# All thirteen steps of a block's attention rows on DVE from block 4 on, in a window attention followed by a SiLU MLP

## The chip, the cores and the metric

The kernel runs on one core of one Trainium2 chip. The metric is the device time of one execution in microseconds, the median of several runs. A core has five engines with queues of their own, each worked off strictly in order: PE (TensorE, with its weight loads as PEld), DVE (VectorE), ACT (ScalarE), POOL (GpSimd) and SP (SyncE, which here only starts DMAs).

## The reference

```python
w = softmax(weight_gen)                 # over 7 taps, per token and head: (4, 4096, 8, 7)
x_pad = 6 zero rows, then x             # (4, 4096, 192), 8 heads of 24 columns
a[s, h] = sum over k of w[s, h, k] * x_pad[s + k, h]       # k = 0 .. 6
h = a @ w_in                            # 192 -> 2048
out = (h * sigmoid(h)) @ w_out          # 2048 -> 192, 16384 tokens
```

The attention rows `a` of one block take seven multiplications (one for each tap, with the softmax weight spread over a head's 24 columns) and six additions: thirteen elementwise operations.

## The kernel before, in words

The 16384 tokens are 128 tiles of 128, worked in 32 blocks of four tiles. Each block goes through eight pairs of hidden slices: 256 blocks-times-pairs in all, numbered through; "pair n" is one of them, and pairs 8b to 8b+7 belong to block b. For each pair there is
- `mm1` on PE (L570): the first product into a PSUM buffer `h`. There are two such buffers, taken in turn.
- `act` on ACT (L582): SiLU in place in `h`; then `upper` on ACT (L593): the high f16 half of it into a ring in SBUF.
- `lower` on DVE (L597): the low f16 half, from `h` and the high half. It is the last reader of `h`; `mm1` of pair n+2 needs it done.
- the second product on PE (L611 for blocks 1 to 5, L636 and L640 from block 6 on), some pairs behind. `mm1` is ahead of it by three pairs at first and by nine at the end (`lead`); where the lead grows by one, two `mm1` follow each other without a second product between them.
- every second pair (from block 6 on) the output steps: L681 on ACT, L682 and L684 on DVE, and a DMA out.

Beside this runs the preparation of later blocks. `prep_steps` (L460) makes the attention rows of a block: multiplications (L472) and additions (L478) on tiles of 128 x 768 f32, then `hi` on ACT (L445) and `lo` on DVE (L448) split the sum into f16 halves, and `turned` lets a DMA transpose them. In blocks 1 to 3 DVE does all thirteen operations. From block 4 on POOL does taps 0 to 2 (three multiplications, two additions) and DVE taps 3 to 6 (four multiplications, three additions) and one addition that brings both sums together: eight on DVE.

The softmax of the weights is made by chunk; from block 4 on a chunk is four blocks. `softmax_steps` (L362): maximum on DVE (L369), subtraction (L372) on POOL, exponential on ACT (L376, with two table loads around it), sum on DVE (L380), reciprocal on DVE (L384, L385), and `norm`, the multiplication with the reciprocal, on POOL (L388). (Chunk 3 has the POOL steps on DVE.)

The order within an engine is written out by hand: `START` gives each preparation step a due time in half pairs, counted from `u0 = (b - 2) * 16` of its block, `chain` enters the steps, and `drain(u)` in the main loop emits what is due, once ahead of a pair's `lower` (even number) and once behind it (odd number). Steps with a fraction are emitted at the next drain.

Of the kernel before, what the change touches and what calls it, by code (L numbers as in the profile page):

```python
# [50 lines left out]
    "any_x": (-39, -27, -15, -11, -4.5, 3, 4, 5),  # L51
    "early": (-5, -41),
    "b3v": (11, 11, 13, 13, 15, 17, 17, 18, 19, 20.5, 20.5, 21, 21, 22.5, 23, 23),
    "b4v": (10, 12, 13, 14.5, 16, 17, 18.5, 20, 22.5, 23, 23),
    "any_p": (11.25,) * 5,
    "any_v": (11, 11.5, 13, 14, 15, 17, 18.5, 20, 22.5, 23, 23),
    "prep": (12.5,),
    "load": (0,),
}
# [19 lines left out]
def kernel(  # L79
# [362 lines left out]
    def split(xs, acc, c, ts):  # L442

        def hi():
            nc.scalar.activation(out=xs[:, ts, 0:D], in_=acc, func=AF.Copy, scale=sc[c, "up"])  # L445

        def lo():
            nc.vector.scalar_tensor_tensor(out=xs[:, ts, D:2 * D], in0=acc, scalar=sc[c, "up"],  # L448
                                           in1=xs[:, ts, 0:D], op0=ALU.mult, op1=ALU.subtract)
        return hi, lo  # L450

    def turned(b, xs):
        def turn():
            xt[b] = xt_p.tile([P, TB, NG, P], F16, tag="xt", name=f"xt{b}")
            nc.sync.dma_start_transpose(out=xt[b].rearrange("p t k n -> p (t k) n"),
                                        in_=xs.rearrange("p t n -> p (t n)"))
            swapped(b, slice(0, TB), (nc.sync, nc.sync))
        return turn

    def prep_steps(b, share):  # L460

        c = chunk_of[b]
        r0 = b * TB - chunks[c][0]
        tags = [0, 1, 1] + [2, 3, 3, 3] if share else [0] + [1 + k % 3 for k in range(K - 1)]
        tiles = [pr_p.tile([P, TB, D], F32, tag=f"pr{n}", name=f"pr{b}_{n}") for n in range(4)]
        pr = [tiles[n] for n in tags]

        def mul(eng, k):
            def f():
                xin = x_t[c][:, r0 + k:r0 + k + TB, :].rearrange("p t (h g) -> p (t h) g", g=G)  # L470
                wv = w_t[c][:, r0 * H:(r0 + TB) * H, k:k + 1].to_broadcast([P, TB * H, G])
                eng.tensor_tensor(out=pr[k].rearrange("p t (h g) -> p (t h) g", g=G),  # L472
                                  in0=xin, in1=wv, op=ALU.mult)
            return f

        def add(eng, k, l):
            def f():
                eng.tensor_tensor(out=pr[k], in0=pr[k], in1=pr[l], op=ALU.add)  # L478
            return f

        def ordered(eng, ks):
            fs = [mul(eng, ks[0])]
            for k in ks[1:]:
                fs += [mul(eng, k), add(eng, ks[0], k)]
            return fs

        pool = ordered(nc.gpsimd, range(share)) if share else []
        steps = ordered(nc.vector, range(share, K)) + ([add(nc.vector, share, 0)] if share else [])
        xs = xs_p.tile([P, TB, 2 * D], F16, tag="xs", name=f"xs{b}")
        hi, lo = split(xs, pr[share % K], c, slice(0, TB))  # L490
        return pool, steps, [hi, lo, turned(b, xs)]
# [210 lines left out]
    def at(u, f):  # L702
        todo.append((u, len(made), f))
        made.append(f)
# [7 lines left out]
    def chain(name, fs, u0=0):  # L712
        steps = START[name][-len(fs):]
        for u, f in zip(steps, fs):
            at(u0 + u, f)

    win, wout = moe_w_in.bitcast(I32), moe_w_out.bitcast(I32)
    with tc.manual_schedule():
# [118 lines left out]
        for c in range(2, NC):  # L837
            u0 = (chunks[c][0] // TB - 2) * NF
# [26 lines left out]
        for b in range(2, NB):  # L865
            u0 = (b - 2) * NF

            def prep(b=b, u0=u0):
                pool, steps, last = prep_steps(b, 0 if b < 4 else 3)
                if b > 2:  # L870
                    chain("any_p", pool, u0)
                chain(f"b{b}v" if b < 5 else "any_v", steps + last, u0)
            at(START["prep"][0] if b == 2 else u0 - 1, prep)

# [101 lines left out]
```

## Time and profile before

| | before |
|---|---|
| median of 3 runs | 1031.17 us (1030.92 to 1033.29) |
| the profiled execution | 1031.08 us, span of its trace 1029.3 us |
| PE busy | 1024.7 us (100% of the span) |
| DVE busy | 788.0 us (77%) |
| ACT busy | 728.3 us (71%) |
| POOL busy | 278.3 us (27%) |

The span runs from the first to the last instruction that the trace shows; 1.8 us of the execution lie around it. Busy shares are averages over the span. A busy PE is not proof of PE at its peak, since the ends of its matmuls are modelled; where PE stands still is seen better from the starts of its instructions. Durations of DVE, ACT and POOL overlap a little: the next one can begin before the end that the trace gives for the last, so what an operation costs its engine is read from start to start.

### The profile page before, as it was taken

To read this page: it belongs to the slowest core of one execution; us is meant where nothing else is said; L and a number is where in the kernel's file an instruction comes from. 1 tells how busy PE (TensorE), PEld (TensorE's weight loads), DVE (VectorE), ACT (ScalarE), POOL (GpSimd) and SP (SyncE) were. 2 spreads that over 40 slices of the span, in tenths; PEclk is the share of its full clock that TensorE was granted. 3 is DMA by queue.
4 is the path that set the end of the run, shared out by engine and by line. 5 is a ranking of instruction groups with operands and counts; after the bars stand their busy time and mean duration, and the time that the engine had idled before them with its cause. 6 is when DMAs were issued, how large, how long until landed. Compare 5 with 4: busy or idle time off the path is not lost.

```text
span 1029.3 us, 30061 instructions
## 1 busy us (share of the span) xinstructions
PE 1024.7 (100%) x13492; PEld 862.9 (84%) x13492; DVE 788.0 (77%) x925; ACT 728.3 (71%) x795; POOL 278.3 (27%) x178
## 2 busy tenths in 40 slices
PE   9999999999999999999999999999999999999998
PEld 7699777788888888888888888888888888888888
DVE  8899866778887777977878778787787877777543
ACT  7988668767786677766787666876668766666662
POOL 1000443433412334312344213343123433123000
PEclk9999999999999999999999999999999999999999
DMA  9441411124112241013221141111312210111100
GB/s 264 138 134 32 151 33 48 48 43 147 15 42 48 50 140 35 22 48 108 82 47 25 32 150 48 39 48 25 134 48 47 41 47 10 47 48 40 47 18 25
DMA packets 71771, 66.74 MB, mean 65 GB/s; under 512 B 51421, under 2 KB 65370, under 8 KB 70618
## 3 DMA queue, kind: packets, MB, share of 16 engines
q1 hardware_dynamic: 71642, 64.83, 23.8%
q8 instruction: 105, 1.72, 0.7%
q14 instruction: 24, 0.20, 0.1%
HBM read 27.85 MB, written 12.58 MB: 39 GB/s over the span
## 4 chain that ended last, share of the span: by engine, by line
PE 99%; DMA 0%; DVE 0%; SPq 0%; issue 0%; ACT 0%; DVEq 0%
PE h L570 47%; PE acc L636 26%; PE acc L640 13%; PE acc L611 8%; PE h L561 2%; PE acc L623 2%; DMA xc<-in_x_dram 0%; PE sum L519 0%; PE acc L649 0%; PE turn L534 0%; DVE pr L513 0%; DVE ringed L528 0%; DVE pr L524 0%; DVE ringed L513 0%; SPq L337 0%
## 5 line engine op out<-in xcount | busy, mean ns | idle before, releaser
L597 DVE SCALAR_TENSOR_TENSOR ringed<-h,gup,ringed 128x1024 f16<-128x1024 f32 x248 | 317.2, 1279 | 213.3 <-ACT ringed L593 213.2
L582 ACT ACTIVATE h<-h,inv 128x1024 f32<-128x1024 f32 x248 | 269.7, 1088 | 266.5 <-PE h L570 264.8
L636 PE MATMUL acc<-wo,ringed 64*128 64x384 f16 x3312 | 433.7, 322 | 0.0
L570 PEld LDWEIGHTS <-w 64*128 64x128 f16 x4464 | 326.1, 94 | 110.0
L640 PE MATMUL acc<-wo,ringed 64*128 64x192 f16 x3312 | 417.7, 243 | 0.0
L570 PE MATMUL h<-xu,w 64*128 64x512 f16 x2232 | 308.4, 376 | 0.0
L570 PE MATMUL h<-xt,w 64*128 64x512 f16 x2232 | 308.4, 376 | 0.0
L593 ACT ACTIVATE ringed<-h,gup 128x1024 f16<-128x1024 f32 x248 | 276.3, 1114 | 8.0
L636 PEld LDWEIGHTS <-ringed 64*128 64x128 f16 x3312 | 259.1, 94 | 20.6
L640 PEld LDWEIGHTS <-ringed 64*128 64x128 f16 x3312 | 259.2, 94 | 11.9
L472 POOL TENSOR_TENSOR pr<-xc,wc 128x768 f32<-128x768 f32 x84 | 136.7, 1641 | 323.5 <-DVE pr L478 227.4
L472 DVE TENSOR_TENSOR pr<-xc,wc 128x768 f32<-128x768 f32 x133 | 129.1, 974 | 1.0
L478 DVE TENSOR_TENSOR pr<-pr,pr 128x768 f32<-128x768 f32 x130 | 128.6, 989 | 0.6
L478 POOL TENSOR_TENSOR pr<-pr,pr 128x768 f32<-128x768 f32 x56 | 111.6, 1993 | 4.4
L611 PEld LDWEIGHTS <-ringed 64*128 64x128 f16 x1920 | 83.9, 94 | 6.1
L611 PE MATMUL acc<-wo,ringed 64*128 64x192 f16 x1920 | 87.7, 243 | 0.0
L682 DVE SCALAR_TENSOR_TENSOR t<-acc,od,t 128x384 f32<-128x384 f32 x103 | 62.7, 609 | 7.8 <-ACT t L681 7.8
L681 ACT ACTIVATE t<-acc,od 128x384 f32<-128x384 f32 x103 | 59.0, 573 | 9.8 <-PE acc L640 9.8
L684 DVE TENSOR_TENSOR o<-t 128x192 f32<-128x192 f32 x103 | 56.1, 545 | 3.6
L448 DVE SCALAR_TENSOR_TENSOR xs<-pr,xup,xs 128x768 f16<-128x768 f32 x31 | 56.5, 1822 | 0.8 <-ACT xs L445 0.8
L388 POOL TENSOR_TENSOR wc<-wc,ws 128x896 f32<-128x896 f32 x6 | 11.1, 1844 | 110.5 <-DVE ws L385 110.5
L372 POOL TENSOR_TENSOR wc<-wc,wm 128x896 f32<-128x896 f32 x6 | 10.5, 1754 | 84.2 <-DVE wm L369 84.2
(101 smaller groups left out, 346.6 us busy)
## 6 DMA issues: line engine op xcount, KB each, us to landing
xc<-in_x_dram SPq DMA_DIRECT2D x7, 2112.0 KB, 9.3
xu<-xt SPq DMA_DIRECT2D x62, 192.0 KB, 3.0
out_dram<-o SPq DMA_DIRECT2D x61, 192.0 KB, 2.7
wc<-in_weight_gen_dram SPq DMA_DIRECT2D x7, 448.0 KB, 3.8
ringed<-in_moe_w_out_dram SPq DMA_DIRECT2D x8, 384.0 KB, 6.8
ringed<-in_moe_w_in_dram SPq DMA_DIRECT2D x14, 192.0 KB, 7.1
xc<-in_x_dram SPq DMA_DIRECT2D x1, 1344.0 KB, 10.5
xc<-in_x_dram SPq DMA_DIRECT2D x2, 384.0 KB, 5.1
```

Of the source, the lines that this page charges most:

```text
L448: nc.vector.scalar_tensor_tensor(out=xs[:, ts, D:2 * D], in0=acc, scalar=sc[c, "up"], in1=xs[:, ts, 0:D], op0=ALU.mult, op1=ALU.subtract)
L472: eng.tensor_tensor(out=pr[k].rearrange("p t (h g) -> p (t h) g", g=G), in0=xin, in1=wv, op=ALU.mult)
L478: eng.tensor_tensor(out=pr[k], in0=pr[k], in1=pr[l], op=ALU.add)
L570: nc.tensor.matmul(h[:, i], w16[rows, part, p, g], x_in[rows, :, k, :], start=n == 0, stop=n == NT9 - 1)
L582: nc.scalar.activation(out=h, in_=h, func=AF.Silu, scale=sc[chunk_of[b], "inv"])
L593: nc.scalar.activation(out=g_t[b, p][:, 0], in_=h_t[b, p], func=AF.Copy, scale=sc[chunk_of[b], "gup"])
L597: nc.vector.scalar_tensor_tensor(out=g[:, 1], in0=h_t.pop((b, p)), scalar=sc[chunk_of[b], "gup"], in1=g[:, 0], op0=ALU.mult, op1=ALU.subtract)
L611: nc.tensor.matmul(acc_t[b, i, t // 2][:, t % 2, :], g[rows, t * P:(t + 1) * P], wo16[rows, place(f), part], start=f == ORDER[0] and t % 2 ...
L636: nc.tensor.matmul(acc_t[b, t, i], gh_t[b, f][rows, t * P:(t + 1) * P], wo16[rows, place(f)], start=f == 0, stop=False, skip_group_check=True)
L640: nc.tensor.matmul(acc_t[b, t, i][:, 0, :], gl_t[b, f][rows, t * P:(t + 1) * P], wo16[rows, place(f), 0], start=False, stop=False, skip_gr ...
L681: nc.scalar.activation(out=t1, in_=acc_t[b, t, 0], func=AF.Copy, scale=sc[c, "od"])
L682: nc.vector.scalar_tensor_tensor(out=t1, in0=acc_t[b, t, 1], scalar=sc[c, "od"], in1=t1, op0=ALU.mult, op1=ALU.add)
```

## The change

From block 4 on `prep_steps(b, 0)` is called instead of `prep_steps(b, 3)`: DVE does the seven multiplications and six additions of a block by itself, as it did in blocks 1 to 3, and POOL none of them. The list of due times for POOL goes, and the two for DVE have sixteen entries (thirteen operations, `hi`, `lo`, `turned`) instead of eleven; the first is 9 instead of 10 or 11, the last three stay. POOL keeps L372, L388 and the maxima over partitions (L166).

```diff
-    "b4v": (10, 12, 13, 14.5, 16, 17, 18.5, 20, 22.5, 23, 23),
-    "any_p": (11.25,) * 5,
-    "any_v": (11, 11.5, 13, 14, 15, 17, 18.5, 20, 22.5, 23, 23),
+    "b4v": (9, 10, 11, 11.5, 13, 13.5, 15, 15.5, 17, 17.5, 19, 19.5, 21, 22.5, 23, 23),
+    "any_v": (9, 10, 11, 11.5, 13, 13.5, 15, 15.5, 17, 17.5, 19, 19.5, 21, 22.5, 23, 23),
...
             def prep(b=b, u0=u0):
-                pool, steps, last = prep_steps(b, 0 if b < 4 else 3)
-                if b > 2:
-                    chain("any_p", pool, u0)
+                _, steps, last = prep_steps(b, 0)
                 chain(f"b{b}v" if b < 5 else "any_v", steps + last, u0)
```

## Rows read from the trace of the kernel before

**Rows 1.** Chain that ended last: share of the span by engine and line.

```profile
PE h L570 47%; PE acc L636 26%; PE acc L640 13%; PE acc L611 8%; PE h L561 2%; PE acc L623 2%; DMA xc<-in_x_dram 0%; PE sum L519 0%; PE acc L649 0%; PE turn L534 0%; DVE pr L513 0%; DVE ringed L528 0%; DVE pr L524 0%; DVE ringed L513 0%; SPq L337 0%
```

**Rows 2.** Page's groups: line, engine, tiles, count, busy us, mean ns, idle before.

```profile
L597 DVE SCALAR_TENSOR_TENSOR ringed<-h,gup,ringed 128x1024 f16<-128x1024 f32 x248 | 317.2, 1279 | 213.3 <-ACT ringed L593 213.2
...
L472 POOL TENSOR_TENSOR pr<-xc,wc 128x768 f32<-128x768 f32 x84 | 136.7, 1641 | 323.5 <-DVE pr L478 227.4
...
L478 POOL TENSOR_TENSOR pr<-pr,pr 128x768 f32<-128x768 f32 x56 | 111.6, 1993 | 4.4
...
L388 POOL TENSOR_TENSOR wc<-wc,ws 128x896 f32<-128x896 f32 x6 | 11.1, 1844 | 110.5 <-DVE ws L385 110.5
```

**Rows 3.** One 31 us stretch: busy PE, PEld, DVE, ACT, POOL; PE clock.

```profile
527.00:558.00 31.00, 31.00 (x401) 26.41 (x398) 26.22 (x28) 25.64 (x28) 9.39 (x6) 1.00 0.22 40
```

**Rows 4.** Timeline near 106 us, PE and DVE: start us, us, instruction.

```profile
104.16 1.24 PE L570 MATMUL h<-xt,w 64*128 64x512 f16 x9
...
106.88 1.28 DVE L597 SCALAR_TENSOR_TENSOR ringed<-h,gup,ringed 128x1024 f16<-128x1024 f32 x1
...
108.21 1.24 PE L570 MATMUL h<-xt,w 64*128 64x512 f16 x9
```

**Rows 5.** Timeline near 118 us, POOL and DVE.

```profile
117.77 2.60 POOL L478 TENSOR_TENSOR pr<-pr,pr 128x768 f32<-128x768 f32 x1
...
118.74 2.45 DVE L478 TENSOR_TENSOR pr<-pr,pr 128x768 f32<-128x768 f32 x1
```

**Rows 6.** Timeline of DVE, 536 to 556 us.

```profile
536.64 1.28 DVE L597 SCALAR_TENSOR_TENSOR ringed<-h,gup,ringed 128x1024 f16<-128x1024 f32 x1 [3.06 <-ACT ringed L593]
...
547.53 1.27 DVE L597 SCALAR_TENSOR_TENSOR ringed<-h,gup,ringed 128x1024 f16<-128x1024 f32 x1
548.72 0.95 DVE L472 TENSOR_TENSOR pr<-xc,wc 128x768 f32<-128x768 f32 x1
549.59 0.22 DVE L384 TENSOR_SCALAR ws<-ws 128x128 f32<-128x128 f32 x1
...
550.71 1.18 DVE L597 SCALAR_TENSOR_TENSOR ringed<-h,gup,ringed 128x1024 f16<-128x1024 f32 x1
551.81 1.70 DVE L478 TENSOR_TENSOR pr<-pr,pr 128x768 f32<-128x768 f32 x1
...
555.22 1.27 DVE L597 SCALAR_TENSOR_TENSOR ringed<-h,gup,ringed 128x1024 f16<-128x1024 f32 x1
```

**Rows 7.** Timeline of PE, 549 to 559 us: starts of the first product.

```profile
549.77 1.24 PE L570 MATMUL h<-xt,w 64*128 64x512 f16 x9
...
553.68 1.24 PE L570 MATMUL h<-xt,w 64*128 64x512 f16 x9
...
557.58 1.24 PE L570 MATMUL h<-xt,w 64*128 64x512 f16 x9
```

**Rows 8.** Timeline of DVE and POOL, 180 to 188 us.

```profile
180.49 1.28 DVE L597 SCALAR_TENSOR_TENSOR ringed<-h,gup,ringed 128x1024 f16<-128x1024 f32 x1
...
183.21 1.28 DVE L597 SCALAR_TENSOR_TENSOR ringed<-h,gup,ringed 128x1024 f16<-128x1024 f32 x1 [0.57 <-ACT ringed L593]
...
185.53 0.95 DVE L385 RECIPROCAL ws<-ws 128x128 f32<-128x128 f32 x1
186.40 0.90 DVE L478 TENSOR_TENSOR pr<-pr,pr 128x768 f32<-128x768 f32 x1
187.21 1.27 DVE L597 SCALAR_TENSOR_TENSOR ringed<-h,gup,ringed 128x1024 f16<-128x1024 f32 x1
...
186.62 2.28 POOL L388 TENSOR_TENSOR wc<-wc,ws 128x896 f32<-128x896 f32 x1 [16.75 <-DVE ws L385]
```

**Rows 9.** Timeline of PE, 182 to 189 us: starts of the first product.

```profile
182.70 1.24 PE L570 MATMUL h<-xt,w 64*128 64x512 f16 x9
...
184.64 1.24 PE L570 MATMUL h<-xt,w 64*128 64x512 f16 x9
...
188.56 1.24 PE L570 MATMUL h<-xt,w 64*128 64x512 f16 x9
```

## The prediction

> **What bounds the kernel now.** I read the chain of waits first: 94% of the span lie in it on PE, in the first matrix product (L570, 47%) and the second (L636, L640 and L611, 26, 13 and 8%) [rows 1]. So a time can only come or go where PE stands still. The page's groups come next: DVE's `lower` (L597), which turns the hidden values into their low halves and by that gives the PSUM buffer `h` back, has idle time of 213.3 us in front of its 248 instructions, all of it spent on ACT, whose `upper` it needs [rows 2]. DVE is therefore not the bound, but 26.22 us of the fullest 31 us are already used [rows 3]. In the steady blocks PE's first product starts every 3.90 us, once a pair (549.77, 553.68, 557.58) [rows 7]; eight pairs are a block, 31.2 us.
>
> The number that decides is how late `lower` may be. There are two `h` buffers, so the first product of pair n+2 cannot start before `lower` of pair n is done. The trace shows the price of that once: `lower` started at 106.88 and took 1.28 us, until 108.16; the first product that needs its buffer started at 108.21, 4.05 us behind the one before, where 3.92 is the pace of that phase (184.64 to 188.56) [rows 4, 9]. So **a `lower` must start 1.33 us before the first product two pairs on**; each later start is time of the kernel, one for one, as PE never catches up.
>
> **The change, part by part.** From block 4 on (28 blocks) GpSimd gives up three multiplications and two additions a block: 84 of 1641 ns and 56 of 1993 ns [rows 2]. They were on no path, so their removal by itself is worth 0. DVE had four multiplications and three additions of its own and one that took in GpSimd's sum, eight; it now has thirteen, five more. What one costs DVE is the distance to the next start: 548.72 to 549.59, **0.87 us** [rows 6]; so 4.35 us a block. The row of thirteen also begins two half pairs earlier (due times 9 and 10 instead of 11), where DVE idles: 3.06 us ahead of the `lower` at 536.64 [rows 6]. The final step, both conversions and the transposing DMA keep their due times (22.5, 23, 23), so nothing is moved past SP's queue and no load waits longer; GpSimd's softmax steps have less in front of them. I cost these at 0.
>
> Of the average alone nothing would follow. A pair now has up to two of these operations beside `lower`, whose step is 548.72 - 547.53 = 1.19: 1.19 + 2 x 0.87 = 2.93 us. Every second pair also has the output's two small steps; in the gap from 550.71 to 555.22 they are what is left, 4.51 less 1.19, less two operations, less 0.75 of waiting (1.70 instead of 0.95), 0.83 us [rows 6]. That is 3.76 and 2.93, and both fit into 7.8 us. The loss comes where a chunk's softmax falls into this: its sum (L380), its reciprocal (L384, L385) on DVE and then its `norm` on GpSimd (L388). L388 runs six times on GpSimd [rows 2], once while the products' lead still grows (near 186 us) and five times in the steady blocks (every fourth block, the one at 551 us being the pattern).
>
> *The five steady ones, at the pattern of 536 to 558 us* [rows 6, 7]. Up to the `lower` before the softmax's sum the gaps hold as many steps as before. Then:
> - The gap with the sum in it gets one more operation: `lower` starts at 547.53 + 0.87 = 548.40. Its limit is 549.77 - 1.33 = 548.44: just held.
> - The gap with the reciprocal gets one more: before it was 550.71 - 547.53 = 3.18, now 4.05, so 548.40 + 4.05 = 552.45. Limit 553.68 - 1.33 = 552.35: 0.10 late.
> - The next gap has as many operations as before, 555.22 - 550.71 = 4.51, which includes the addition that stood 1.70 us instead of 0.95 behind `norm`: 556.96. Limit 557.58 - 1.33 = 556.25: **0.71 late**, with the 0.10 in it. The pair behind has one operation and no output, and the lateness is gone.
>
> Five times 0.71 = 3.55 us.
>
> *The one near 186 us* [rows 8, 9]. Here two first products follow each other directly (182.70, 184.64), so the `lower` in front has hardly any room.
> - One operation more ahead of the `lower` at 180.49: 181.36; limit 182.70 - 1.33 = 181.37: held.
> - Then 1.19 + 2 x 0.87 (before: one operation and 0.57 of idling): 184.29 instead of 183.21. Limit 184.64 - 1.33 = 183.31: **0.98 late**.
> - The addition that stood between that `lower` and the reciprocal now stands behind it, so the reciprocal starts 1.19 and 0.26 later (0.26 for L384 is what 185.53 - 183.21 leaves beside 1.19 and 0.87), at 185.74, and the addition at 186.61. `norm` asks 1.09 behind the reciprocal's start (186.62 - 185.53), that is at 186.83, while the addition runs; before, it ended 2.50 behind the addition's start (186.62 + 2.28 - 186.40), so now at 189.11. The new multiplication, next on DVE, waits for that, and `lower`, queued behind it, starts at 189.98. Limit 188.56 + 0.98 - 1.33 = 188.21: **1.77 late**.
>
> Together 2.75 us. That the multiplication waits is read from a pattern: an addition of GpSimd that was held until a DVE operation ended (2.60 us, from 117.77) ran first, and DVE's next addition stood 2.45 us from 118.74 [rows 5]: whoever asked first got its turn. Were DVE's queue served through instead, the multiplication would not wait from 187.48 to 189.11, `lower` would start at 188.35, and the stop would be 0.14: 1.12 in place of 2.75 us. That is the lower bound of this part.
>
> What is the bound of an added operation? Its step is 0.81 in the shortest row (186.40 to 187.21) [rows 8] and 0.95 if nothing of it overlapped the next (its own duration at 548.72) [rows 6]. With two added ones before the limit, a steady event costs 0.59 to 0.87, five 2.95 to 4.35. I take 0.87 because five of the six places have just this neighbourhood. [...]
>
> **Sum.** 3.55 + 2.75 = 6.3 us on the profiled execution's own time, 1031.08 us (span 1029.3); that execution is 0.09 us below the median of 1031.17. Prediction: 1031.1 + 6.3 = **1037.4 us**, +0.6%. About 0.3%, 3.1 us, is what a measurement of this kernel tells from no change. In all other blocks (no sum or reciprocal) I forecast no stop.
>
> **The rivals.**
> - *The reserve holds (not slower).* The limits are missed by tenths, so a few tenths decide. If each steady event is missed by 0.2 instead of 0.71 (the two `lower`s then start half a microsecond earlier, because ACT and DVE stand a little differently to each other) and `norm` comes behind the multiplication, the sum is 5 x 0.2 + 1.1 = 2.1: 1033.2 us, within 0.3%. For it: the first limits are held by 0.04 and 0.01 only on paper, and GpSimd's multiplications and additions, which held up DVE elsewhere [rows 5], go away. Against it: in the events walked through the only wait for GpSimd is that for `norm`, and that stays. It decides as soon as an event costs under 0.4 us.
> - *DVE falls behind in more places.* If the added operations take 0.95 and more and the ordinary pairs with output then start a softmax event already late by 0.4 us, each steady event costs 0.71 + 0.4 = 1.1, and the one near 186 us 2.75 + 0.4 = 3.2: 5 x 1.1 + 3.2 = 8.7: 1039.8 us. For it: such a pair needs 3.76 of 3.90 us. Against it: the neighbour pair has 0.97 us over, so lateness does not add up. A permanent backlog would need over 31.22 us of DVE in a block; 26.22 + 4.35 in the fullest slice is 30.6, and that still counts the waits on GpSimd that go.
> - *Faster.* DVE gets rid of GpSimd as a neighbour. PE waits for it almost nowhere now (0.13 us in the place of rows 4), so hardly half a microsecond can come of it: 1030.6 us, within 0.3%.
>
> **How the numbers follow.** Forecast (over 1034.3): 0.70; reserve holds: 0.20; falls behind further: 0.08; gain: 0.02, which I leave whole to "faster". So slower 0.78, same 0.20, faster 0.02. The forecast's own range, from the bounds of both parts, is 2.95 + 1.12 = 4.1 to 4.35 + 2.75 = 7.1, 1035.2 to 1038.2; to hold 8 in 10 it must reach into both neighbours: 1033.0 to 1041.0.
>
> **What would show it.** GpSimd without L472 and L478. PE with stops in front of L570, five of some 0.7 us, at a spacing of four blocks (125 us), and two of about 1 and 2 us near 185 and 190 us; between them a distance of 3.90 us, unchanged. A DVE multiplication of some 2.5 us behind `norm` near 187 us. I am wrong if PE shows no stop there, if it shows stops in blocks without a softmax sum, or if the granted clock falls below 1.0 behind a stop: the stretch of rows 3, in which PE works without a break, has 1.00 [rows 3], and no row here shows what a stop of 2 us does to it.

## The result: 1042.64 us, 1.1% slower, and the profile after

| | before | after |
|---|---|---|
| median | 1031.18 us (4 runs) | 1042.64 us (4 runs, 1042.07 to 1043.73) |
| the profiled execution | 1031.08 us, span 1029.3 us | 1042.07 us, span 1040.3 us |
| DVE busy | 788.0 us | 863.2 us |
| POOL busy | 278.3 us | 32.3 us |

The ratio is 1.0113, with an interval of 1.0102 to 1.0125. The direction is the forecast one, but the time lies 5.2 us above the predicted 1037.4 and 1.6 us above the upper end of the range.

The lines of L471, L477, L387, L569, L596 of the kernel after are L472, L478, L388, L570, L597 of the one before: between the two places of the change lines stand one lower, behind the second three. The page's busy times and the chain of work that ended last, after:

```profile
PE 1027.1 (99%) x13492; PEld 710.5 (68%) x13492; DVE 863.2 (83%) x1065; ACT 728.4 (70%) x795; POOL 32.3 (3%) x38
...
PE 85%; DVE 9%; issue 3%; ACT 2%; DMA 1%; SPq 0%; DVEq 0%; POOL 0%; ACTq 0%
```

Where PE carried nearly all of the chain before [rows 1], 9% of it now lie on DVE and 3% on "issue". Such a share is not time lost, since the chain runs on along DVE from each point at which DVE held PE up. Where PE stood still is in the view of its waits (engine, tile and line, what it waited for: us in total, times, longest):

```profile
PE sum L518 <- POOL ident masks.py:199: 4.5, 1, 4.5
PE h L569 <- DVE ringed L596: 4.0, 7, 1.5
```

Before, neither of the two stood in that view. The second is the forecast one: seven stops of `mm1` behind `lower`, five and two. The first was in no step of the prediction: the first products behind the opening's row of `cold` products wait 4.5 us for GpSimd to finish the identity matrix.

*What the seven stops cost.* I compared the starts of SiLU every eight pairs between the traces. The blocks in which no softmax ends take as long as before (31.22 us in the steady stretch). The five with a steady event take 31.75, so 0.53 each, 2.65 together; the one near 191 us takes 29.92 where it took 27.44, so 2.48. That is 5.13 us for the seven stops; by the starts of SiLU they cost more than the 4.0 us of idle time in the view of waits, as the ends of PE's instructions, from which that view counts, are modelled. One more block, the second, has 0.14 over (31.67 for 31.53), which makes 5.27 us. It is an eighth late `lower`, too small to show as a wait: behind the `norm` of chunk 3, which DVE does itself (L387 at 113.76 us), there now stand two multiplications where there was one,

```profile
116.63 1.28 DVE L596 SCALAR_TENSOR_TENSOR ringed<-h,gup,ringed 128x1024 f16<-128x1024 f32 x1
```

```profile
117.96 1.24 PE L569 MATMUL h<-xt,w 64*128 64x512 f16 x9
```

and `mm1` follows 1.33 behind it, 4.06 behind the `mm1` before it, where it was 3.92 (108.21 to 112.13 in the kernel before). Timelines of DVE and of PE, around the first steady event and around the one at 191 us, with GpSimd's `norm` of the latter (start, us, instruction, idle time before it and what ended that):

```profile
187.18 1.27 DVE L596 SCALAR_TENSOR_TENSOR ringed<-h,gup,ringed 128x1024 f16<-128x1024 f32 x1
...
190.11 1.28 DVE L596 SCALAR_TENSOR_TENSOR ringed<-h,gup,ringed 128x1024 f16<-128x1024 f32 x1
...
192.42 0.90 DVE L477 TENSOR_TENSOR pr<-pr,pr 128x768 f32<-128x768 f32 x1
193.23 2.50 DVE L471 TENSOR_TENSOR pr<-xc,wc 128x768 f32<-128x768 f32 x1
195.66 1.27 DVE L596 SCALAR_TENSOR_TENSOR ringed<-h,gup,ringed 128x1024 f16<-128x1024 f32 x1
...
300.23 0.95 DVE L477 TENSOR_TENSOR pr<-pr,pr 128x768 f32<-128x768 f32 x1
301.10 0.95 DVE L471 TENSOR_TENSOR pr<-xc,wc 128x768 f32<-128x768 f32 x1
...
306.81 1.27 DVE L596 SCALAR_TENSOR_TENSOR ringed<-h,gup,ringed 128x1024 f16<-128x1024 f32 x1
...
310.86 1.18 DVE L596 SCALAR_TENSOR_TENSOR ringed<-h,gup,ringed 128x1024 f16<-128x1024 f32 x1
311.96 1.70 DVE L477 TENSOR_TENSOR pr<-pr,pr 128x768 f32<-128x768 f32 x1
...
315.37 1.28 DVE L596 SCALAR_TENSOR_TENSOR ringed<-h,gup,ringed 128x1024 f16<-128x1024 f32 x1
```

```profile
192.65 2.27 POOL L387 TENSOR_TENSOR wc<-wc,ws 128x896 f32<-128x896 f32 x1 [33.02 <-DVE ws L384]
```

```profile
191.44 1.24 PE L569 MATMUL h<-xt,w 64*128 64x512 f16 x9 [0.79 <-DVE ringed L596]
...
196.99 1.24 PE L569 MATMUL h<-xt,w 64*128 64x512 f16 x9 [1.45 <-DVE ringed L596]
...
312.26 1.24 PE L569 MATMUL h<-xt,w 64*128 64x512 f16 x9
...
316.70 1.24 PE L569 MATMUL h<-xt,w 64*128 64x512 f16 x9 [0.35 <-DVE ringed L596]
```

The reader should lay these beside [rows 6] and [rows 8]. The gaps between the steady `lower`s are the forecast ones: 310.86 - 306.81 = 4.05 and 315.37 - 310.86 = 4.51; and `mm1` starts 316.70 - 315.37 = 1.33 behind the late `lower`, the limit that [rows 4] gave, here and at 191.44 - 190.11 and 196.99 - 195.66. From 312.26 to 316.70 are 4.44 us, where the pace is 3.90. Near 191 us the DVE multiplication behind the reciprocal and one addition stands 2.50 us, beside `norm`, as forecast.

*What the opening costs.* The first SiLU of block 1 starts at 62.35 us; before, at 56.66. That is 5.69 us, and 5.69 + 5.27 = 10.96 is the whole difference of the spans, 11.0. Timelines of GpSimd and of PE from the start, after:

```profile
1.71 0.19 POOL masks.py:197 MEMSET ident<- 128x128 f32 x1
9.63 0.28 POOL masks.py:199 TENSOR_SCALAR_AFFINE_SELECT ident<-ident 128x128 f32<-128x128 f32 x1 [7.72 <-DMA ringed<-in_moe_w_in_dram]
...
820.50 1.02 POOL L165 PARTITION_ALL_REDUCE mb_x<-xm  x1 [6.01 <-ACT xs L444]
```

```profile
9.96 4.21 PE L518 MATMUL sum<-ringed,ident 128*128 128x384 f32 x6 [4.49 <-POOL ident masks.py:199]
...
16.33 0.98 PE L533 MATMUL turn<-ident,ringed 128*128 128x128 f32 x6 [0.65 <-DVE ringed L527]
```

and of the same places before:

```profile
2.21 0.28 POOL masks.py:199 TENSOR_SCALAR_AFFINE_SELECT ident<-ident 128x128 f32<-128x128 f32 x1 [0.31 <-POOL ident masks.py:197]
...
935.63 2.40 POOL L478 TENSOR_TENSOR pr<-pr,pr 128x768 f32<-128x768 f32 x1
```

```profile
6.29 2.41 PE L519 MATMUL sum<-ringed,ident 128*128 128x384 f32 x6
...
10.64 0.99 PE L534 MATMUL turn<-ident,ringed 128*128 128x128 f32 x6 [0.65 <-DVE ringed L528]
```

GpSimd's instructions up to here are the same, in the same order, in both kernels. Yet the selection that writes the identity comes 7.42 us later, PE starts 3.67 us later (9.96 against 6.29), and by the `turn` product it is 5.69 us late. The last 2.02 us come while PE already has its data: six products take 4.21 us instead of 2.41, and the four behind them 1.72 instead of 1.45. The table of stretches has the granted clock for it, after, and in its last row that for the two stops near 191 us (us, busy PE, PEld, DVE, ACT, POOL with counts, then the granted clock of PE as a share, the DMA share and GB/s):

```profile
7.50:10.00 2.50, 0.04 (x1) 0.04 (x1) 0.00 (x0) 1.07 (x3) 0.31 (x2) 0.53 1.00 252
10.00:12.50 2.50, 2.50 (x4) 1.47 (x5) 1.85 (x4) 0.02 (x1) 2.13 (x9) 0.50 0.98 324
12.50:15.00 2.50, 2.50 (x6) 1.33 (x5) 1.41 (x3) 0.00 (x0) 0.66 (x2) 0.60 1.10 273
15.00:20.00 5.00, 4.35 (x25) 2.46 (x24) 4.09 (x9) 3.27 (x8) 0.00 (x0) 1.00 1.08 280
190.00:200.00 10.00, 7.75 (x116) 5.30 (x114) 9.88 (x10) 7.23 (x8) 2.27 (x1) 1.00 0.00 0
```

PE was idle from about 5.5 us to 9.96; from 10 to 12.5 us the clock stood at 0.50, the level of 1.2 GHz, and it was back at 1.00, 2.4 GHz, from 15 us on. Before, all these stretches have 1.00.

The releaser in brackets, a DMA of `ringed`, can't be the cause: nothing in the selection reads that tile. Up to this row GpSimd's queue is the same in both kernels; what differs, besides the work between, is its end: its last instruction is a TENSOR_TENSOR before, and a PARTITION_ALL_REDUCE after, since the change took away the additions behind it. That gave the theory for the experiments.

### The profile page after: what moved, and what is told of

The parts are those of the page before. It is cut to its first block, busy times and chain, and to the rows that moved or that the text cites. A ratio compares the mean times of both kernels' runs of the same rounds, so it can differ in the third digit from the quotient of the medians.

```text
span 1040.3 us, 30027 instructions
## 1 busy us (share of the span) xinstructions
PE 1027.1 (99%) x13492; PEld 710.5 (68%) x13492; DVE 863.2 (83%) x1065; ACT 728.4 (70%) x795; POOL 32.3 (3%) x38
## 3 DMA queue, kind: packets, MB, share of 16 engines
q8 instruction: 105, 1.72, 0.7%
## 4 chain that ended last, share of the span: by engine, by line
PE 85%; DVE 9%; issue 3%; ACT 2%; DMA 1%; SPq 0%; DVEq 0%; POOL 0%; ACTq 0%
PE h L569 40%; PE acc L635 22%; PE acc L639 11%; PE acc L610 7%; DVE pr L477 3%; DVE pr L471 3%; DVE ringed L596 2%; PE h L560 2%; PE acc L622 2%; DVE t L681 1%; PE sum L518 1%; ACT ringed L592 1%; ACT h L581 1%; DVE ws L379 1%; DMA xc<-in_x_dram 0%
## 5 line engine op out<-in xcount | busy, mean ns | idle before, releaser
L596 DVE SCALAR_TENSOR_TENSOR ringed<-h,gup,ringed 128x1024 f16<-128x1024 f32 x248 | 317.5, 1280 | 144.7 <-ACT ringed L592 144.3
L639 PE MATMUL acc<-wo,ringed 64*128 64x192 f16 x3312 | 409.1, 243 | 0.0
L569 PEld LDWEIGHTS <-w 64*128 64x128 f16 x4464 | 253.9, 94 | 187.3 <-issue 5.3
L569 PE MATMUL h<-xt,w 64*128 64x512 f16 x2232 | 308.4, 376 | 4.0 <-DVE ringed L596 4.0
L569 PE MATMUL h<-xu,w 64*128 64x512 f16 x2232 | 308.4, 376 | 0.0
L635 PEld LDWEIGHTS <-ringed 64*128 64x128 f16 x3312 | 187.9, 94 | 91.9
L471 DVE TENSOR_TENSOR pr<-xc,wc 128x768 f32<-128x768 f32 x217 | 205.4, 958 | 0.1
L639 PEld LDWEIGHTS <-ringed 64*128 64x128 f16 x3312 | 187.9, 94 | 20.5
L477 DVE TENSOR_TENSOR pr<-pr,pr 128x768 f32<-128x768 f32 x186 | 183.8, 988 | 0.5
L610 PEld LDWEIGHTS <-ringed 64*128 64x128 f16 x1920 | 83.3, 94 | 6.6
L610 PE MATMUL acc<-wo,ringed 64*128 64x192 f16 x1920 | 87.3, 243 | 0.0
L683 DVE TENSOR_TENSOR o<-t 128x192 f32<-128x192 f32 x103 | 36.9, 358 | 3.6
L444 ACT ACTIVATE xs<-pr,xup 128x768 f16<-128x768 f32 x31 | 28.8, 928 | 7.4 <-DVE pr L477 7.3
L495 ACT ACTIVATE junk<-xc 128x960 int8<-128x960 f32 (+2 forms) x29 | 32.5, 1121 | 0.0
L447 DVE SCALAR_TENSOR_TENSOR xs<-pr,xup,xs 128x768 f16<-128x768 f32 x31 | 31.2, 1006 | 0.8 <-ACT xs L444 0.8
L622 PEld LDWEIGHTS acc<-v_out,ringed 64*128 64x128 f32 x256 | 21.5, 187 | 2.0 <-issue 1.6
```

The source lines that it names most:

```text
L569: nc.tensor.matmul(h[:, i], w16[rows, part, p, g], x_in[rows, :, k, :], start=n == 0, stop=n == NT9 - 1)
L596: nc.vector.scalar_tensor_tensor(out=g[:, 1], in0=h_t.pop((b, p)), scalar=sc[chunk_of[b], "gup"], in1=g[:, 0], op0=ALU.mult, op1=ALU.subtract)
L610: nc.tensor.matmul(acc_t[b, i, t // 2][:, t % 2, :], g[rows, t * P:(t + 1) * P], wo16[rows, place(f), part], start=f == ORDER[0] and t % 2 ...
L622: nc.tensor.matmul(acc_t[0, i, t // 2][:, t % 2, :], gh_t[0, f][rows, t * P:(t + 1) * P], v_out[rows, p, f // NP], start=f == 0 and t % 2 ...
L635: nc.tensor.matmul(acc_t[b, t, i], gh_t[b, f][rows, t * P:(t + 1) * P], wo16[rows, place(f)], start=f == 0, stop=False, skip_group_check=True)
L639: nc.tensor.matmul(acc_t[b, t, i][:, 0, :], gl_t[b, f][rows, t * P:(t + 1) * P], wo16[rows, place(f), 0], start=False, stop=False, skip_gr ...
```

## Experiments

**Theory.** GpSimd must set itself up anew when the kind of its work changes between PARTITION_ALL_REDUCE and the elementwise instructions, and what it is set up for at the end of one execution is what the next one finds. So the kernel after pays in its opening for its own last instruction. **Rivals:** the opening is late for another reason (the changed program, its transfers), whatever ends the queue; or anything at all behind the reduction would do. For the stops of `mm1` the theory is that of the prediction, and the rival, that DVE is simply too full.

### A small elementwise instruction at the end of GpSimd's queue

The kernel after, with two GpSimd instructions on a tile of their own behind all others:

```diff
+        tail = const.tile([P, 2], F32, name="tail")
+        nc.gpsimd.memset(tail, 0.0)
+        nc.gpsimd.tensor_tensor(out=tail[:, 0:1], in0=tail[:, 0:1], in1=tail[:, 1:2], op=ALU.add)
```

> The changed kernel with one small GpSimd TENSOR_TENSOR (and a memset for its inputs) as the last thing on GpSimd's queue, behind the last PARTITION_ALL_REDUCE at 820 us, where nothing waits for it. Theory A (GpSimd starts an execution set up for the kind of instruction that the previous execution ended with; with a PARTITION_ALL_REDUCE last, the AFFINE_SELECT of the identity waits 7.7 us in the opening): the wait falls back to 0.3 us as before, PE's wait of 4.5 us and its 6.8 us at half clock go, the first SiLU of block 1 starts at 56.7 instead of 62.35, and the time is 1042.6 - 5.7 = 1037.0 us. Theory B (the opening waits for something that comes in by DMA at that moment, as the releaser named in the trace says, or for the fetch of a GpSimd program that is now laid out otherwise): a few instructions at the end change nothing, 1042.6 us.

Measured: 1036.44 us (ratio to before 1.0051, 1.0034 to 1.0068). GpSimd's timeline:

```profile
2.21 0.28 POOL masks.py:199 TENSOR_SCALAR_AFFINE_SELECT ident<-ident 128x128 f32<-128x128 f32 x1 [0.31 <-POOL ident masks.py:197]
...
815.08 1.09 POOL L165 PARTITION_ALL_REDUCE mb_x<-xm  x1 [5.94 <-ACT xs L444]
816.05 0.16 POOL L943 MEMSET tail<- 128x2 f32 x1
823.20 0.32 POOL L944 TENSOR_TENSOR tail<-tail 128x1 f32<-128x1 f32 x1 [6.98 <-issue]
```

The selection is back at 2.21 us, the first SiLU at 56.97, and 6.2 us of the loss are gone, for an instruction of 0.32 us at 823 us. The last row shows what the theory calls the set-up, as a wait: the addition depends on nothing but the memset in front of it, and yet stands 6.98 us away from it, with no releaser but "issue". Here that costs nothing, as nobody waits for it. The seven stops are all there: PE still waits 4.0 us in seven places for L596, and the blocks' times are 31.75 and 29.93.

### The reverse: a small reduction at the end of the kernel before

The kernel before, with the same memset and, in place of the addition,

```diff
+        nc.gpsimd.partition_all_reduce(tail[:, 0:1], tail[:, 1:2], P, bass_isa.ReduceOp.max)
```

> The kernel before with one small PARTITION_ALL_REDUCE (and a memset) as the last thing on GpSimd's queue. Nothing else is changed and nothing waits for it. Theory A: the AFFINE_SELECT of the next execution waits some 7.7 us, PE 4.5 us, and the time is 1031.2 + 5.7 = 1036.9 us. Theory B: 1031.2 us, unchanged.

Measured: 1037.64 us (1.0061, 1.0046 to 1.0076). GpSimd's timeline, and PE's waits:

```profile
10.39 0.28 POOL masks.py:199 TENSOR_SCALAR_AFFINE_SELECT ident<-ident 128x128 f32<-128x128 f32 x1 [8.49 <-DMA ringed<-in_moe_w_in_dram]
...
945.06 0.10 POOL L946 MEMSET tail<- 128x2 f32 x1
951.34 0.52 POOL L947 PARTITION_ALL_REDUCE tail<-tail  x1 [6.18 <-issue]
```

```profile
PE sum L519 <- POOL ident masks.py:199: 4.3, 1, 4.3
```

The kernel before, none of whose own instructions were touched, loses 6.45 us by the medians (1031.19 beside it) through what stands at its end. In the profiled execution it is 7.1 us of the span (1036.4 against 1029.3), all in the opening: the first SiLU is at 63.75 against 56.66, 7.09 us. So the end of GpSimd's queue decides the opening in both directions, and the change's own loss there is not an effect of the work that moved to DVE. That the end of one execution hands its state to the next is the reading that fits; no trace shows the handing over.

### Only the memset at the end

The kernel after with the first two added lines alone.

> The changed kernel with one small GpSimd MEMSET as the last thing on its queue, the control for the last but one. Theory A, in the form that a memset needs no set-up of its own (in the opening the memsets ran at 0.7 and 1.7 us, ahead of the wait): 1042.6 us, unchanged. If any instruction behind the last PARTITION_ALL_REDUCE helps: 1037.0 us. Theory B: 1042.6 us.

Measured: 1042.97 us (1.0111, 1.0096 to 1.0126), as the kernel after. GpSimd's timeline:

```profile
9.97 0.28 POOL masks.py:199 TENSOR_SCALAR_AFFINE_SELECT ident<-ident 128x128 f32<-128x128 f32 x1 [8.06 <-DMA ringed<-in_moe_w_in_dram]
...
822.37 0.16 POOL L943 MEMSET tail<- 128x2 f32 x1
```

A memset at the end repairs nothing, so it is not the presence of something behind the reduction that counts. It also starts at once behind the reduction (821.37 + 1.12 = 822.49) and does not wait as the addition did: in the terms of the theory, a memset needs no new set-up and makes none.

### The softmax steps later, away from the tight pairs

The kernel after, with the sum, the reciprocal and `norm` of a chunk entered one to six half pairs later, so that they fall where DVE has room:

```diff
-    "any_s": (-32, -32, -23, -16, -14, -10),
-    "c4s": (-32, -32, -19, -16, -13, -10),
+    "any_s": (-32, -32, -23, -10, -8, -7),
+    "c4s": (-32, -32, -19, -13, -10, -9),
```

> The changed kernel with the softmax's sum, reciprocal and norm moved to pairs in which DVE has no attention step ahead of lower (due -10, -8, -7 instead of -16, -14, -10; for chunk 4 -13, -10, -9 instead of -16, -13, -10). Theory (the six stops of PE come from these steps lying in pairs that have two attention steps already): the stops of 0.53 us, five times, and of 2.5 us near 191 to 197 us go, 5.2 us in all, and the opening stays as late: 1042.6 - 5.2 = 1037.4 us. Rival (DVE with all thirteen steps is too full anywhere): the stops move with the steps and the time stays within 1 us of 1042.6.

Measured: 1037.11 us (1.0057, 1.0042 to 1.0072). All waits of PE:

```profile
PE sum L518 <- POOL ident masks.py:199: 4.6, 1, 4.6
PE cold L733 <- DVE zero L721: 1.0, 1, 1.0
PE turn L533 <- DVE ringed L527: 0.7, 1, 0.7
```

The line for L596 is gone, and the blocks with a softmax take 31.22 us again (27.45 near 191 us). DVE does exactly the same operations, so it was not too full: the seven stops came only from where the softmax steps stood among the thirteen. The 0.14 us of the second block stay (31.67 again), as the due times of chunk 3 were not touched. The opening's wait is untouched, so the two losses don't depend on each other.

### Both repairs at once

> Both repairs together: the changed kernel with the softmax's sum, reciprocal and norm at the new due times and one small TENSOR_TENSOR at the end of GpSimd's queue. If the two losses are separate and there is no third, they add up: 1042.6 - 5.7 - 5.2 = 1031.7 us, no difference from the kernel before (1031.2) that can be measured. If the retimed steps only hid behind the late opening, or DVE is too full for another reason, it stays at 1034 us or above.

The retimed softmax steps and the addition at the end together. Measured: 1031.20 us against 1030.94 for the kernel before, run beside it (1.0003, 0.9994 to 1.0012). The span is 1029.3 us, that of before. With both causes taken away nothing that can be told from the noise is left of the 11 us (the 0.14 of the second block still stand in the trace); nothing is gained either, since in both kernels PE is all but gapless. The 246 us of GpSimd's time that the change frees reach no one.

### `norm` of chunk 4 on DVE

To price the stop near 191 us by its parts: the kernel with the addition at the end, and the one `norm` that the crowded multiplication waits for done by DVE:

```diff
-            eng.tensor_tensor(out=w, in0=w, in1=s["s"][:, 0:n].unsqueeze(2).to_broadcast([P, n, K]),
+            (nc.vector if c == 4 else eng).tensor_tensor(out=w, in0=w, in1=s["s"][:, 0:n].unsqueeze(2).to_broadcast([P, n, K]),
```

> The changed kernel with the small TENSOR_TENSOR at the end of GpSimd's queue, and the norm of chunk 4 (the one near 186 us) on DVE, due a pair later than the reciprocal, with all due times as in the change. Theory (PE's second stop there, 1.45 us by the trace, is DVE's multiplication held by GpSimd's norm until that has ended): no multiplication of 2.5 us there, the first stop of 0.79 stays, the second is 0.2 or less, and the time is 1036.4 - 1.5 = 1034.9 us. Rival (the stop comes from the number of DVE steps alone, the wait for norm is covered): the second stop stays or grows by norm's 1.0 us on DVE, 1036.4 to 1037.4 us.

Measured: 1035.09 us (1.0040, 1.0026 to 1.0054); the block takes 28.37 instead of 29.93. DVE's timeline, and PE's waits:

```profile
187.81 0.94 DVE L471 TENSOR_TENSOR pr<-xc,wc 128x768 f32<-128x768 f32 x1
188.68 1.28 DVE L596 SCALAR_TENSOR_TENSOR ringed<-h,gup,ringed 128x1024 f16<-128x1024 f32 x1
```

```profile
PE h L569 <- DVE ringed L596: 2.6, 6, 0.8
```

The multiplication takes 0.94 us instead of 2.50, exactly the 1.56 us that the block gets back, and one of the seven stops is gone. The first of the two near 191 us stays (0.80 us): it belongs to the second added operation ahead of the `lower`, not to `norm`. The Trainium skill ("SBUF — State Buffer", Who interferes with whom) has DVE and GpSimd share one pair of SBUF ports as an exclusive lock. The rows here agree with it: beside `norm`, which ran to 194.92, the multiplication stood until 195.73, 2.50 us, and without `norm` 0.94; no row shows the lock itself.

## Why the prediction was wrong, point by point

- **The failing step** is "They were on no path, so their removal by itself is worth 0". I looked for what the removed instructions held up within an execution, and they held up nothing. I did not ask what they left behind for the next one. They kept a TENSOR_TENSOR as the last instruction of GpSimd's queue; without them it is a PARTITION_ALL_REDUCE, and by the experiments with the end of that queue this is what makes the opening late: 5.69 us of the span (6.2 to 6.5 us by the medians: 1042.64 and 1042.97 without the addition at the end, 1036.44 with it). With that term the sum would have been 1037.4 + 5.7 = 1043.1 us; measured 1042.6. That "slower" came out as forecast rests on the stops; the opening's half of the loss was not foreseen at all.
- The trace of before had a sign of it that I passed over. Its GpSimd timeline has, right behind the additions of a block,

```profile
196.09 1.81 POOL L478 TENSOR_TENSOR pr<-pr,pr 128x768 f32<-128x768 f32 x1
203.68 0.66 POOL L166 PARTITION_ALL_REDUCE mb_x<-xm  x1 [5.78 <-issue]
214.54 3.05 POOL L472 TENSOR_TENSOR pr<-xc,wc 128x768 f32<-128x768 f32 x2 [10.19 <-issue]
```

  a reduction that stands 5.78 us with no releaser, at each of the later chunks too (5.8 to 6.2 us, put down to whatever had last come in). That a change of kind may take GpSimd some 6 us could be read there; that the end of the queue bears on the next execution, no row of one execution can show.
- **The limit law was right**: 1.33 us between the late `lower` and `mm1`, at all four places shown. So were the places (five stops four blocks apart, two near 191 us), the steady pace between them, and the granted clock, 1.00 from 190 to 200 us although PE stands for 2.2 us there.
- **The steady event was mis-sized**: 0.54 us at its `mm1` (4.44 for 3.90), not 0.71. The forecast put the `lower` behind the sum 0.87 us later than in the kernel before. There it starts at 297.77 at the same place; with the 8.34 us by which `mm1` is late by then (312.26 against 303.92) that is 306.98, and it came at 306.81, 0.17 sooner. Of this, 0.11 lie in one step of the row of thirteen, from an addition to the next multiplication: 0.98 us in the kernel before,

```profile
541.70 0.95 DVE L478 TENSOR_TENSOR pr<-pr,pr 128x768 f32<-128x768 f32 x1
542.68 0.96 DVE L472 TENSOR_TENSOR pr<-xc,wc 128x768 f32<-128x768 f32 x1
```

  and 301.10 - 300.23 = 0.87 after; why it was longer before is in no row. The rest comes in steps of some hundredths. 0.71 - 0.17 = 0.54 is the stop as measured. All five: 2.65 against 3.55 us.
- **The event near 191 us was right to within a tenth of its size**: 2.48 us by its block against 2.75. Its two stops are 0.98 and 1.63 by the starts of `mm1`, forecast 0.98 and 1.77; the block gets a little of that back, as one pair behind them took 4.00 us before (192.49 to 196.49) and 3.92 after. With the 5.82 us that the kernel is late there, the forecast `lower`s are at 181.36 + 5.82 = 187.18 and 184.29 + 5.82 = 190.11, which is where they stand; the last came at 195.66 instead of 195.80. That the multiplication would wait behind `norm`, 2.5 us, was read from [rows 5] and held.
- **A seventh place was left out**: the 0.14 us of the second block. The prediction walked through the six softmaxes whose `norm` is on GpSimd; that of chunk 3, with `norm` on DVE, met the earlier start of the row of thirteen too. By the prediction's own figures this could be read: the `lower` 0.87 later, at 110.07 + 0.87 = 110.94, and its limit 112.13 - 1.33 = 110.80.
- **The rivals.** "The reserve holds" is out: `norm` came first, and the events cost 0.53. "DVE falls behind in more places" gave 1039.8, nearer to the result by its number, and is out too: but for the 0.14 us of the second block, the blocks without a softmax's end take as long as before, and DVE had more room than I gave it. It does 131.5 us more of multiplications and additions (76.3 in L471 and 55.2 in L477), but its busy time grew by only 75.2. Of the 56.3 us between, 44.5 are in two groups whose instructions became shorter once GpSimd's additions and multiplications were gone, here after:

```profile
L683 DVE TENSOR_TENSOR o<-t 128x192 f32<-128x192 f32 x103 | 36.9, 358 | 3.6
...
L447 DVE SCALAR_TENSOR_TENSOR xs<-pr,xup,xs 128x768 f16<-128x768 f32 x31 | 31.2, 1006 | 0.8 <-ACT xs L444 0.8
```

  Their means were 545 and 1822 ns: 103 x 0.187 = 19.2 and 31 x 0.816 = 25.3 us. "Faster" is out: with both losses repaired the kernel is at 1031.20 us, so this room on DVE is off PE's path.
- **The size of an added operation** was the forecast 0.87 us (300.23 to 301.10, with a duration of 0.95).

## What to carry to other kernels

When instructions are taken from GpSimd, look at what then stands last on its queue and what stands first in the next execution, not only at who waited for them. Take idle time with no releaser, or with one whose tile the instruction doesn't touch, for a possible cost of the engine itself, and see who would wait if it fell elsewhere. Where the bound engine is nearly gapless, a few added microseconds on another one cost only where short events meet: move those events first. Here their due times alone gave back all that the seven stops had cost.

## What the runs showed of the hardware that was not expected

- GpSimd pays for a change of kind: 6.18 us of standing from a memset to a PARTITION_ALL_REDUCE when TENSOR_TENSORs came before, 6.98 us to a TENSOR_TENSOR behind a reduction and a memset; the memset neither pays nor changes it. What is set up in that time is in no row. The Trainium skill ("GPSIMD Engine Reference", 2.1 Instruction dispatch) tells of some 6 us, with no instruction visible, at the first call of a freshly loaded GpSimd kernel. The 6.18 and 6.98 us agree with that in size, but they stand in the middle of an execution, at changes of kind; that they are such a load is not shown.
- It seems to outlive the execution: the last instruction on GpSimd's queue, at 820 to 951 us and with nobody waiting for it, decides whether the first selection of an execution starts at 2.21 or at 9.63 to 10.39 us. This is concluded from kernels that differ only at the end of the queue, not seen directly; that the end of the program instead changes how the next start is prepared, outside the trace, is not ruled out.
- A wait of 4.5 us in the opening costs PE more than its length: 3.67 us of later start and 2.02 us at a granted clock of 0.50 to 0.60. That split is read from the one trace; no run tested the two apart. The stops of 0.8 and 1.5 us near 191 us left the clock at 1.00.
